# Attention probabilities scaled on VectorE or ScalarE instead of GpSimd, with a re-timed list schedule

## The chip, the cores and the metric

One core of a Trainium2 chip runs the whole kernel. The metric is the device time of one execution in microseconds (us); the time before is the median of three runs. The core's engines are TensorE (PE in the profile, its weight loads PEld), VectorE (DVE), ScalarE (ACT), GpSimd (POOL) and SyncE (SP), which issues most DMAs.

## The reference

Block-causal attention, then two MLPs over the same 2304 tokens, all in float32:

```python
# q, k, v: (4 batches, 8 heads, 576 positions, 64)
scores = scale * np.matmul(q, k.transpose(0, 1, 3, 2))
mask = block_i >= block_j                    # blocks of 64 positions
scores = np.where(mask, scores, -1000000000.0)
scores = scores - np.max(scores, axis=-1, keepdims=True)
attn = np.exp(scores)
attn = attn / (np.sum(attn, axis=-1, keepdims=True) + 1e-09)
x = np.matmul(attn, v)                       # -> (2304, 512)
h = x @ w_in;  r = np.maximum(h, 0.0);  g = s * (r * r) + b;  x = g @ w_out    # first MLP, d_ff 2048
h = x @ w_in2; g = np.maximum(0.01 * h, h);  out = g @ w_out2                  # second MLP, d_ff 2048
```

## The kernel before

The 576 positions are cut into five query tiles of 128 (the last one 64), over all four batches: tile `k` gives the first MLP a block of 512 tokens (tile 4: 256). They are taken in the order 0, 1, 2, 4, 3. While the first MLP works on one block (16 slices `f` of the hidden layer; `m_in` writes `h` with the matmuls of L910, `m_out` accumulates `y` with those of L953), the attention of the next block runs between its matmuls (`later_block`). So up to about 520 us TensorE has two streams of work; then the last block runs alone, and from about 592 us the second MLP, with seven products in place of eight for each pair of blocks (L1166 into the hidden layer, L1231 out of it).

Float32 matmuls of the MLPs are done as three with operands split into a high and a low part (`xh`, `xl`, `gh`, `gl`, and for weights `w`). VectorE and ScalarE split weights and activations, evacuate PSUM, and do the softmax. The weights of the second MLP are split and combined in slots named `unit` during the first one (L457 to L477).

One attention step of `later_block` takes one batch and one pair of heads, 16 steps for each of the four later tiles:

- TensorE: scores into PSUM (`s`; L577 for tile 1, L782 for tiles 2 and 3, L822 for tile 4).
- VectorE: row maximum; ScalarE: exponential with the sum of each row into `l`; VectorE: adds 1e-9 and takes the reciprocal (L556, L799, L840).
- The scaling, which multiplies each row of `P` by its value in `l`, in place: L569 for tile 1 (two instructions a step, 192 and 256 columns), L801 for tiles 2 and 3 (two a step, 384 or 512 columns), L841 for tile 4 (one a step, 576 columns). Before the change it may run on GpSimd or VectorE. Tile 0 scales on VectorE with a broadcast product (L562).
- TensorE: transposes of `P` in groups of four into `t` (L592); VectorE or ScalarE evacuates them into `pt`, part of the buffer `pv` (`evac`, L508 on ScalarE, L510 on VectorE); TensorE: the product with V (L861).

The order of all instructions on all engines is written out by a list scheduler in the kernel's own code, class `Graph`. Each operation is added as a step with the engines that may run it and a duration on each (`act`, `dve`, `pool`), its predecessors, the buffers that it opens and uses, and a due time. `Graph.order` simulates the engines: whenever an engine is idle in this simulation it takes the ready step with the earliest due time. Steps are then issued in the simulated order, and each engine works through its own queue in order; what waits at run time waits by semaphore. `LAT` is the time from a step's end until those who wait for it are ready in the simulation, `AGAIN` by how much an engine is free earlier than its step's end, `TURN` the cost on TensorE of a change between full, row-tiled and column-tiled matmuls. Steps marked `port` on VectorE and GpSimd exclude each other in the simulation.

Of the kernel before, what the change touches and what calls it, by code (L numbers as in the profile page):

```python
# [43 lines left out]
class Graph:  # L44
    LAT = 0.04
    AGAIN = {"DVE": 0.08, "ACT": 0.09, "POOL": 0.05}
# [8 lines left out]
    def add(self, eng, fn, after=(), opens=(), uses=(), due=0.0, port=False, nbytes=0, rel=0.0, mode="f", behind=(), run=2048):  # L55
        s = Step(eng, fn, after, opens, uses, due, port, nbytes)
        s.rel = rel
        s.mode = mode
        s.wire = nbytes / abs(run) * (12.0 + abs(run) / 23.0) / 16e3
# [31 lines left out]
    def order(self):  # L91
# [17 lines left out]
        while events:  # L109
            t = events[0][0]  # L110
            while events and events[0][0] <= t:
                _, _, what, s, e = heapq.heappop(events)
                if what == "ready":
                    for x in s.eng:
                        ready[x].append(s)
                elif what == "room":
                    room[s] += 1
                elif what == "free":
                    idle[e] = True
                    if port is s:  # L120
                        port = None
                else:
                    out_there -= s.nbytes > 0
                    for b in s.uses:
                        b.users -= 1
                        if not b.users:
                            heapq.heappush(events, (t + self.LAT, n, "room", b.key, None))
                            n += 1
                    for q in s.succs:
                        q.left -= 1  # L130
                        if not q.left:
                            heapq.heappush(events, (max(t + (0.18 if "POOL" in q.eng and len(q.eng) == 1 else self.LAT), q.rel), n, "ready", q, None))
                            n += 1
            for e in idle:
# [71 lines left out]
def kernel(  # L206
# [135 lines left out]
    def decode(raw, w0, w1, out, n, after, due):  # L342
# [10 lines left out]
        a = G.add({"DVE": dve(n, 2)}, low, after, uses=[raw], due=due, port=True)  # L353
        b = G.add({"ACT": act(n)}, up, after, uses=[raw], due=due)
        return G.add({"DVE": dve(n)}, shift, [a, b], uses=[raw], due=due, port=True)

    def chunk(w, raw, f, lds, halves, due):
# [13 lines left out]
        a = G.add({"DVE": dve(512 * n)}, lo, [a], uses=[w, raw], due=due, port=True)  # L371
# [53 lines left out]
    def units(which, stored):  # L425
# [4 lines left out]
        for n, (half, kind, i) in enumerate(seq[first[which]:first[which + 1]]):  # L430
# [34 lines left out]
            a = G.add({"DVE": dve(1024, 2)}, low, lds, uses=[slot], due=due, port=True)  # L465
            b = G.add({"ACT": act(1024)}, up, lds, uses=[slot], due=due)
            a = G.add({"DVE": dve(1024)}, shift, [a, b], uses=[slot], due=due, port=True)

            def comb(out, x, y, op, after, blk=blk, slot=slot, due=due):
                return G.add({"DVE": dve(256)}, lambda e: e.tensor_tensor(out=blk(out), in0=blk(x), in1=blk(y), op=op), after, uses=[slot], due=due, port=True)  # L470
# [6 lines left out]
            lo = G.add({"DVE": dve(1792)}, lambda e, c7=c7, h7=h7: e.tensor_tensor(out=c7(), in0=c7(), in1=h7(), op=ALU.subtract), [hi], uses=[slot], due=due, port=True)  # L477
# [43 lines left out]
    def softmax(k, banks, cols, P, pcols, due, after):  # L521
# [36 lines left out]
        if k == 0:  # L558
            for j in range(0, ns, 4):
# [4 lines left out]
                out += [G.add({"DVE": dve(n)}, fn, [a], uses=[P, l], due=due - 2.5, port=True)] * 4  # L564
            return out
        for j, (bk, c, n) in enumerate(cols):
            def fn(e, j=j, n=n):
                pp = P()[:, pcols[j]:pcols[j] + n]
                e.tensor_scalar(out=pp, in0=pp, scalar1=l()[:, j:j + 1], scalar2=1.0, op0=ALU.mult, op1=ALU.mult)  # L569
            out.append(G.add({"POOL": pool(n), "DVE": dve(n, 2)}, fn, [a], uses=[P, l], due=due - 2.5, port=True))  # L570
        return out

    def scores(k, q, kk, cols, q_ap, k_ap, after, due, fresh):
        out = []
        for j, (bk, c, n) in enumerate(cols):
# [4 lines left out]
            out.append(G.add({"PE": max(n * 1.67e-3, 0.214) - 0.06}, fn, after, new, [bk, *q, *kk], due - 5))  # L580
# [78 lines left out]
    for p in range(NP):  # L659
# [26 lines left out]
        a = G.add({"PE": 0.208 * 4}, av, [*tr, fv_ok, pads], [o], [pt, fv] + [spare] * (p > 1), due, mode="c")  # L686
# [14 lines left out]
    def score_parts(Q, K, nk, ql, kl, due):  # L701
# [7 lines left out]
            out=kl_()[:, :nk], in0=K()[:, :nk], in1=kh()[:, :nk].bitcast(F32), op=ALU.subtract), [c], [kl_], [K, kh], due=due - 7, port=True)  # L709
        return kh, kl_, qs, [a, c]  # L710

    def later_block(blk):
# [8 lines left out]
        for u in range(NP * B):  # L721
# [48 lines left out]
            if flat:  # L770
# [16 lines left out]
                for h in range(2):  # L787
# [7 lines left out]
                    for h in range(2)  # L795
# [16 lines left out]
            else:  # L812
# [6 lines left out]
                for j in range(2):  # L819
# [21 lines left out]
                nrm = [G.add({"POOL": pool(nk), "DVE": dve(nk, 2)}, lambda e, l=l, P=P: e.tensor_scalar(  # L841
                    out=P()[:, :nk], in0=P()[:, :nk], scalar1=l()[:, 0:1], scalar2=1.0, op0=ALU.mult, op1=ALU.mult), [a], uses=[P, l], due=due - 2.5, port=True)]
# [27 lines left out]
            a = G.add({"PE": many * nj * 0.206 * n / 128}, av, [x for c in pair for x in c[3]], [o] + [xf] * (pair[0][0] == 0), [xf, *[x for c in pair for x in (c[2], c[4])]], due, mode="c")  # L870
# [12 lines left out]
    def x_split(blk, c):  # L883
# [10 lines left out]
            [hi], [l], [h, xf], due, port=True,  # L894
# [5 lines left out]
    def m_in(blk, f, pos):  # L900
# [19 lines left out]
        def square(e):  # L920
# [9 lines left out]
            out=gl()[:, :T], in0=g()[:, :T], in1=gh()[:, :T].bitcast(F32), op=ALU.subtract), [hi], [gl], [g, gh], due, port=True)  # L930
# [112 lines left out]
    x2 = {}  # L1043

    def x_part(j, r, x, after, t):
# [3 lines left out]
        x2[j, r][2] = a = G.add({"DVE": dve(2 * NH)}, lambda e: sub(e, lo(), x(), hi().bitcast(F32)), [a], [lo], [hi, x.buf], t, port=True)  # L1049
# [26 lines left out]
    def x_comb(x, y, z, after, t):  # L1076
        return G.add(tt(2 * NH), lambda e: sub(e, x(), y(), z()), after, [], [x.buf, y.buf, z.buf], t, port=True)
# [110 lines left out]
    def out_phase(n):  # L1188
# [13 lines left out]
        for o, r in enumerate(IN_ORDER):  # L1202
            z, first = where[r]
            for i in range(4):
# [5 lines left out]
                def comb(x, y, w, after):  # L1210
                    return G.add(tt(NH), lambda e: sub(e, x(), y(), w()), after, [], [x, y, w], due - 4, port=True)
# [13 lines left out]
                lo = G.add({"DVE": dve(NH)}, lambda e, gh=gh, gl=gl, x=x: sub(e, gl(), x(), gh().bitcast(F32)), [hi], [gl], [gh, x], due - 1.5, port=True)  # L1225
# [101 lines left out]
```

## Time and profile before

| | |
|---|---|
| median of 3 runs | 957.47 us (957.29 to 958.84) |
| the profiled execution's own time | 957.85 us |
| its span, first to last instruction | 956.1 us |
| TensorE busy | 939.0 us (98%) |
| VectorE, ScalarE, GpSimd busy | 67%, 58%, 11% |
| mean granted TensorE clock | 0.998 |

The profile comes from one execution; durations and waits below are those of that execution. Busy time of TensorE is the time covered by at least one matmul; matmuls are pipelined and their ends are modelled, so one matmul's shown duration runs on over the start of the next. A weight load (PEld) overlaps the matmul in front of it. A wait is idle time of an engine, put down to what ended it.

### The profile page before, as it was taken

How to read it: one execution, taken by the hardware profiler on the slowest of the kernel's cores; microseconds unless marked ns; L12 is line 12 of the kernel's file. 1: busy time of each engine (PE TensorE's matmuls, PEld its weight loads, DVE VectorE, ACT ScalarE, POOL GpSimd, SP SyncE). 2: the span in 40 equal slices, each digit the busy share in tenths (PEclk: the TensorE clock that was granted, in tenths of full speed). 3: DMA queues.
4: the chain of work that ended last, by engine and by line, in shares of the span. 5: the costliest groups of instructions: out<-in, count | busy, mean ns of one | idle time of the engine just before them, and what ended most of it. 6: DMA issues, size and time to landing. Idle time of an engine off the chain costs nothing.

```text
span 956.1 us, 16595 instructions
## 1 busy us (share of the span) xinstructions
PE 939.0 (98%) x5780; PEld 827.9 (87%) x5780; DVE 635.9 (67%) x1300; ACT 559.0 (58%) x1186; POOL 101.4 (11%) x223
## 2 busy tenths in 40 slices
PE   9999999999999999999999999999999999999998
PEld 8778787777778888888887888999999999999998
DVE  5977668866768756666676754556595565855557
ACT  4867657656766745565567643454556646555443
POOL 1122211211121211121220000000000000000000
PEclk9999999999999999999999999999999999999999
DMA  8986677998679885178336992997219852157402
GB/s 226 322 294 221 233 256 249 313 281 243 186 217 336 223 261 173 47 247 236 100 103 206 387 332 87 360 418 322 97 57 322 316 189 99 51 177 292 165 1 67
DMA packets 147668, 208.27 MB, mean 218 GB/s; under 512 B 23552, under 2 KB 118400, under 8 KB 140928
## 3 DMA queue, kind: packets, MB, share of 16 engines
q1 hardware_dynamic: 145136, 206.42, 65.0%
q10 hardware_dynamic: 2448, 0.79, 0.4%
q8 instruction: 46, 0.75, 0.3%
q14 instruction: 38, 0.31, 0.1%
HBM read 154.47 MB, written 52.69 MB: 217 GB/s over the span
## 4 chain that ended last, share of the span: by engine, by line
PE 80%; DMA 6%; DVE 6%; ACT 3%; issue 2%; POOL 2%; SPq 0%; POOLq 0%; DVEq 0%; ACTq 0%
PE y L953 16%; PE h L910 15%; PE A L1231 10%; PE A L1166 10%; PE C L1166 5%; PE C L1231 5%; PE t L592 4%; PE o L861 4%; PE B L1231 3%; PE B L1166 2%; DMA pv<-in_v_dram 2%; PE s L577 2%; PE s L782 2%; PE warm L614 1%; DMA u_in<-unit 1%
## 5 line engine op out<-in xcount | busy, mean ns | idle before, releaser
L910 PE MATMUL h<-xh,w 128*128 128x512 f32 (+1 forms) x640 | 231.5, 388 | 1.7 <-DVE g L924 1.0
L953 PE MATMUL y<-gh,w 128*128 128x512 f32 (+1 forms) x640 | 187.4, 376 | 0.2
L910 PEld LDWEIGHTS h<-xh,w 128*128 128x128 f32 x640 | 119.2, 189 | 28.2 <-issue 5.1
L953 PEld LDWEIGHTS y<-gh,w 128*128 128x128 f32 x640 | 114.0, 189 | 21.3 <-issue 0.9
L1224 ACT ACTIVATE gh<-G 128x384 fp32r<-128x384 f32 x168 | 86.9, 525 | 55.4 <-PE A L1231 21.0
L953 PE MATMUL y<-gl,w 128*128 128x512 f32 (+1 forms) x320 | 118.7, 371 | 0.1
L910 PE MATMUL h<-xl,w 128*128 128x512 f32 (+1 forms) x320 | 118.7, 371 | 0.0
L1166 PE MATMUL A<-xh,wi 128*128 128x384 f32 x384 | 112.4, 336 | 0.0
L1038 DVE TENSOR_TENSOR gl<-G,gh 128x384 fp32r<-128x384 f32 x168 | 91.3, 555 | 29.9 <-ACT gh L1224 28.2
L1231 PE MATMUL A<-gh,wo 128*128 128x384 f32 x384 | 98.0, 336 | 1.4 <-DVE Y L1146 1.4
L926 ACT ACTIVATE g<-h 128x512 f32<-128x512 f32 (+1 forms) x80 | 44.2, 552 | 91.3 <-PE h L910 91.2
L592 PE MATMUL t<-id_sb,p 128*128 128x128 f32 x400 | 68.6, 280 | 8.1 <-POOL p L569 2.7
L592 PEld LDWEIGHTS t<-id_sb,p 128*128 128x128 f32 x400 | 46.6, 140 | 30.6 <-POOL p L569 6.4
L1166 PEld LDWEIGHTS A<-xh,wi 128*128 128x128 f32 x384 | 70.6, 188 | 1.1 <-ACT G L1141 0.9
L1231 PEld LDWEIGHTS A<-gh,wo 128*128 128x128 f32 x384 | 69.1, 188 | 2.4 <-DVE Y L1146 2.3
L953 PEld LDWEIGHTS y<-gl,w 128*128 128x128 f32 x320 | 60.4, 189 | 11.1 <-DVE gl L929 0.7
L929 DVE TENSOR_TENSOR gl<-g,gh 128x512 fp32r<-128x512 f32 (+1 forms) x80 | 53.2, 664 | 22.8 <-ACT gh L928 17.3
L910 PEld LDWEIGHTS h<-xl,w 128*128 128x128 f32 x320 | 60.7, 190 | 7.3
L1180 ACT ACTIVATE G<-G 128x384 f32<-128x384 f32 x72 | 37.6, 524 | 47.8 <-DVE G L1146 47.7
L1166 PE MATMUL A<-xl,wi 128*128 128x384 f32 x192 | 64.4, 335 | 0.0
L1231 PE MATMUL A<-gl,wo 128*128 128x384 f32 x192 | 64.2, 334 | 0.0
L1038 DVE TENSOR_TENSOR G<-G 128x384 f32<-128x384 f32 x96 | 53.1, 555 | 12.3 <-ACT G L1180 10.8
(123 smaller groups left out, 1797.2 us busy)
## 6 DMA issues: line engine op xcount, KB each, us to landing
wi<-u_in SPq DMA_DIRECT2D x32, 896.0 KB, 7.1
wo<-u_out SPq DMA_DIRECT2D x28, 1024.0 KB, 7.4
w<-kept SPq DMA_DIRECT2D x16, 1024.0 KB, 8.0
u_in<-unit SPq DMA_DIRECT2D x16, 896.0 KB, 5.4
u_out<-unit SPq DMA_DIRECT2D x32, 448.0 KB, 5.3
early<-in_moe_w_in_dram SPq DMA_DIRECT2D x16, 512.0 KB, 5.4
early<-in_moe_w_out_dram SPq DMA_DIRECT2D x16, 512.0 KB, 6.4
kept<-w SPq DMA_DIRECT2D x8, 1024.0 KB, 6.6
```

Of the source, the lines that this page charges most:

```text
L577: e.matmul(out=bk()[:, c:c + n], lhsT=q_ap(j), rhs=k_ap(j, n), start=True, stop=True)
L592: e.transpose(tb()[:, x * 128:(x + 1) * 128], P()[:, pc:pc + 128], id_sb)
L861: e.matmul(out=o()[64 * h:64 * h + 64, n * x:n * x + n], lhsT=V()[:, j, 64 * h:64 * h + 64], rhs=r, start=(j == 0), stop=(j == nj - 1),)
L910: e.matmul(out=h()[:, :T], lhsT=w()[:, wi, c * 128:(c + 1) * 128], rhs=x[blk, c]()[:, :T], start=(c == 0 and n == 0), stop=(c == KD - 1 an ...
L926: a = G.add({"ACT": act(T)}, lambda e: e.activation(out=g()[:, :T], in_=h()[:, :T], func=ACTF.Relu), [prev], [g], [h], due)
L929: lo = G.add({"DVE": dve(T)}, lambda e: e.tensor_tensor(out=gl()[:, :T], in0=g()[:, :T], in1=gh()[:, :T].bitcast(F32), op=ALU.subtract), [ ...
L953: e.matmul(out=y()[:, :W], lhsT=w()[:, wi, d * 128:(d + 1) * 128], rhs=x()[:, :W], start=(pos == 0 and n == 0), stop=(pos == NF - 1 and n ...
L1038: e.tensor_tensor(out=out, in0=x, in1=y, op=ALU.subtract)
L1166: e.matmul(out=x()[:, :NH], lhsT=in_w[n, i, c]()[:, s, ai], rhs=y()[:, c], start=(first and c == 0 and m == 0), stop=(c == 1 and m == 2), ...
L1180: {"ACT": act(NH)}, lambda e, y=y: e.activation(out=y(), in_=y(), func=ACTF.Prelu, alpha=0.01), [a], [], [y], d2 + 2)
L1224: hi = G.add({"ACT": act(NH)}, lambda e, gh=gh, x=x: e.activation(out=gh(), in_=x(), func=ACTF.Copy), [a], [gh], [x], due - 2)
L1231: e.matmul(out=z[d]()[:, :NH], lhsT=out_w[n, r]()[:, 2 * i + d, s], rhs=y(), start=(first and i == 0 and m == 0), stop=(i == 3 and m == 2) ...
```

## The change

The scaling of tiles 1 to 4 no longer has GpSimd as a choice: it becomes `evac(e, P, P, l)`, which is a `tensor_scalar` with one multiplication on VectorE, or a Copy activation with `l` as its per-partition scale on ScalarE, with the durations of the new function `norm`. The scheduler takes whichever of the two is idle in its simulation. All `port=True` marks are dropped. In the scheduler, `LAT` depends on the engine that the waiting step goes to; a result of TensorE reaches other engines `LAG` later than it reaches TensorE's own next steps, which follow with no latency; a landed load counts 0.1 us; the durations of the score matmuls and of the products with V are longer. (`tail` is not set by any step.)

```diff
-    LAT = 0.04
-    AGAIN = {"DVE": 0.08, "ACT": 0.09, "POOL": 0.05}
+    LAT = {"PE": 0.055, "DVE": 0.035, "ACT": 0.035, "POOL": 0.17, "SP": 0.03, "X": 0.0}
+    LAG = 0.165
+    AGAIN = {"DVE": 0.08, "ACT": 0.095, "POOL": 0.03}
...
                         if not b.users:
-                            heapq.heappush(events, (t + self.LAT, n, "room", b.key, None))
+                            heapq.heappush(events, (t + 0.036, n, "room", b.key, None))
...
                     for q in s.succs:
+                        if e == "PE" and q.on_pe:
+                            continue
                         q.left -= 1
                         if not q.left:
-                            heapq.heappush(events, (max(t + (0.18 if "POOL" in q.eng and len(q.eng) == 1 else self.LAT), q.rel), n, "ready", q, None))
+                            lat = 0.1 if s.nbytes and not q.nbytes else self.LAT[min(q.eng)]
+                            heapq.heappush(events, (max(t + lat, q.rel), n, "ready", q, None))
...
+                if e == "PE":
+                    for q in s.succs:
+                        if q.on_pe:
+                            q.left -= 1
+                            if not q.left:
+                                heapq.heappush(events, (max(end, q.rel), n, "ready", q, None))
+                                n += 1
+                    end += self.LAG
+                elif e in ("ACT", "DVE") and s.tail:
+                    end += s.tail
...
 def act(n, ptr=0, acc=False):
-    return 0.2 + n / 1200 + 0.14 * acc
+    return 0.205 + n / 1195 + 0.125 * acc
...
+def norm(n):
+    return {"DVE": 0.212 + n / 1840, "ACT": act(n) + 0.06}
...
                 pp = P()[:, pcols[j]:pcols[j] + n]
-                e.tensor_scalar(out=pp, in0=pp, scalar1=l()[:, j:j + 1], scalar2=1.0, op0=ALU.mult, op1=ALU.mult)
-            out.append(G.add({"POOL": pool(n), "DVE": dve(n, 2)}, fn, [a], uses=[P, l], due=due - 2.5, port=True))
+                evac(e, pp, pp, l()[:, j:j + 1])
+            out.append(G.add(norm(n), fn, [a], uses=[P, l], due=due - 2.5))
...
-            out.append(G.add({"PE": max(n * 1.67e-3, 0.214) - 0.06}, fn, after, new, [bk, *q, *kk], due - 5))
+            out.append(G.add({"PE": max(n * 1.67e-3, 0.19) + 0.005}, fn, after, new, [bk, *q, *kk], due - 5))
...
-        a = G.add({"PE": 0.208 * 4}, av, [*tr, fv_ok, pads], [o], [pt, fv] + [spare] * (p > 1), due, mode="c")
+        a = G.add({"PE": 0.218 * 4}, av, [*tr, fv_ok, pads], [o], [pt, fv] + [spare] * (p > 1), due, mode="c")
...
-                    G.add({"POOL": pool(nk), "DVE": dve(nk, 2)}, lambda e, h=h, l=l, P=P: e.tensor_scalar(
-                        out=P()[:, nk * h:nk * h + nk], in0=P()[:, nk * h:nk * h + nk], scalar1=l()[:, h:h + 1], scalar2=1.0, op0=ALU.mult, op1=ALU.mult),
-                        [a], uses=[P, l], due=due - 2.5, port=True)
+                    G.add(norm(nk), lambda e, h=h, l=l, P=P: evac(
+                        e, P()[:, nk * h:nk * h + nk], P()[:, nk * h:nk * h + nk], l()[:, h:h + 1]), [a], uses=[P, l], due=due - 2.5)
...
-                nrm = [G.add({"POOL": pool(nk), "DVE": dve(nk, 2)}, lambda e, l=l, P=P: e.tensor_scalar(
-                    out=P()[:, :nk], in0=P()[:, :nk], scalar1=l()[:, 0:1], scalar2=1.0, op0=ALU.mult, op1=ALU.mult), [a], uses=[P, l], due=due - 2.5, port=True)]
+                nrm = [G.add(norm(nk), lambda e, l=l, P=P: evac(
+                    e, P()[:, :nk], P()[:, :nk], l()[:, 0:1]), [a], uses=[P, l], due=due - 2.5)]
...
-            a = G.add({"PE": many * nj * 0.206 * n / 128}, av, [x for c in pair for x in c[3]], [o] + [xf] * (pair[0][0] == 0), [xf, *[x for c in pair for x in (c[2], c[4])]], due, mode="c")
+            a = G.add({"PE": many * nj * 2 * (0.109 if n == 128 else 0.058)}, av, [x for c in pair for x in c[3]], [o] + [xf] * (pair[0][0] == 0), [xf, *[x for c in pair for x in (c[2], c[4])]], due, mode="c")
```

The other lines of the diff only drop `port=True`, on the subtractions, combinations and weight decoding of VectorE.

## Rows read from the trace of the kernel before

**Rows 1.** The page: engines (busy us, share, instructions); its costliest group (busy, mean ns).

```profile
PE 939.0 (98%) x5780; PEld 827.9 (87%) x5780; DVE 635.9 (67%) x1300; ACT 559.0 (58%) x1186; POOL 101.4 (11%) x223
...
L910 PE MATMUL h<-xh,w 128*128 128x512 f32 (+1 forms) x640 | 231.5, 388 | 1.7 <-DVE g L924 1.0
```

**Rows 2.** Windows: length, busy us (instructions) of each engine, PEclk, DMA share, GB/s.

```profile
25.00:525.00 500.00, 489.25 (x3273) 395.39 (x3272) 356.71 (x795) 322.14 (x699) 96.67 (x205) 1.00 0.72 225
525.00:592.00 67.00, 67.00 (x297) 55.47 (x296) 39.60 (x55) 32.67 (x46) 0.00 (x0) 1.00 0.77 271
592.00:952.00 360.00, 358.63 (x2048) 355.23 (x2047) 225.38 (x421) 191.92 (x386) 0.00 (x0) 1.00 0.54 198
...
50.00:75.00 25.00, 22.86 (x123) 18.40 (x122) 18.95 (x35) 16.43 (x31) 5.49 (x12) 0.93 0.87 291
```

**Rows 3.** Waits of PE: who for whom, total us, times, longest.

```profile
PE t L592 <- POOL p L569: 2.7, 4, 1.6
PE t L592 <- POOL p L801: 2.5, 6, 0.8
...
PE h L910 <- DVE g L924: 1.0, 2, 0.6
...
PE t L592 <- ACT pv L508: 0.3, 1, 0.3
...
PE t L592 <- POOL p L841: 0.2, 1, 0.2
```

**Rows 4.** Waits of PEld, the weight loads, same columns.

```profile
PEld t L592 <- POOL p L569: 6.4, 12, 1.8
PEld t L592 <- POOL p L801: 6.1, 13, 1.0
...
PEld t L592 <- POOL p L841: 2.9, 8, 0.6
```

**Rows 5.** Groups of POOL by shape: count, busy us, mean ns, idle before, releasers.

```profile
L801 POOL TENSOR_SCALAR p<-p,l 128x512 f32<-128x512 f32 x31 | 22.1, 724 | 77.7 <-DVE l L799 65.5 <-ACT xh L891 6.9 <-PE h L910 5.3
L801 POOL TENSOR_SCALAR p<-p,l 128x384 f32<-128x384 f32 x32 | 22.1, 702 | 82.9 <-DVE l L799 57.1 <-ACT gh L928 19.1 <-ACT xf L508 6.7
L841 POOL TENSOR_SCALAR p<-p,l 128x576 f32<-128x576 f32 x16 | 13.6, 847 | 39.6 <-DVE l L840 38.3 <-ACT kh L707 1.3
L569 POOL TENSOR_SCALAR p<-p,l 128x192 f32<-128x192 f32 x15 | 10.1, 675 | 51.3 <-DVE l L556 39.8 <-ACT xh L891 6.0 <-ACT unit L460 4.9
L569 POOL TENSOR_SCALAR p<-p,l 128x256 f32<-128x256 f32 x16 | 10.0, 628 | 0.0
```

**Rows 6.** Lines 569 and 801 by themselves: ns min/median/max, first and last start.

```profile
L569 POOL TENSOR_SCALAR p<-p,l x31: 427/482/1965, 41.8 to 152.3; 128x256 f32<-128x256 f32 x16, 128x192 f32<-128x192 f32 x15
...
L801 POOL TENSOR_SCALAR p<-p,l x63: 582/694/1633, 158.5 to 506.2; 128x384 f32<-128x384 f32 x32, 128x512 f32<-128x512 f32 x31
```

**Rows 7.** Groups of DVE by shape: the two scalings that ran there.

```profile
L801 DVE TENSOR_SCALAR p<-p,l 128x512 f32<-128x512 f32 x1 | 0.5, 491 | 0.0
L569 DVE TENSOR_SCALAR p<-p,l 128x192 f32<-128x192 f32 x1 | 0.3, 312 | 0.0
```

**Rows 8.** Groups of ACT by shape: copies with a per-partition scale, out of PSUM.

```profile
L508 ACT ACTIVATE yo<-y,s_sb 128x512 f32<-128x512 f32 x8 | 5.5, 684 | 3.0 <-PE y L953 2.9
...
L508 ACT ACTIVATE yo<-y,s_sb 128x256 f32<-128x256 f32 x2 | 0.9, 460 | 0.0
```

**Rows 9.** Timeline from 54 us: start, us, engine and instruction, idle before it.

```profile
54.40 2.37 POOL L569 TENSOR_SCALAR p<-p,l 128x192 f32<-128x192 f32 x2 [4.65 <-DVE l L556]
54.67 1.23 DVE L367 TENSOR_TENSOR w<-early,w 128x1024 fp32r<-128x1024 f32 x1
...
56.83 0.55 PE L592 MATMUL t<-id_sb,p 128*128 128x128 f32 x3 [1.61 <-POOL p L569]
```

**Rows 10.** The chain that ended last, from 542 us: start, us, what.

```profile
542.87 3.40 PE h L910 x15
```

**Rows 11.** Groups of DVE by shape: the longest instruction of the weight split.

```profile
L477 DVE TENSOR_TENSOR unit<-unit 128x1792 f32<-128x1792 f32 x16 | 32.5, 2032 | 11.3 <-ACT unit L476 11.2
```

More of the change, by code (lines that the diff above doesn't have):

```diff
@@ L53, in __init__, with add @@
         self.room, self.inturn, self.steps, self.gates = room, inturn, [], {}
-    def add(self, eng, fn, after=(), opens=(), uses=(), due=0.0, port=False, nbytes=0, rel=0.0, mode="f", behind=(), run=2048):
+    def add(self, eng, fn, after=(), opens=(), uses=(), due=0.0, port=False, nbytes=0, rel=0.0, mode="f", behind=(), run=2048, tail=0.0):
         s = Step(eng, fn, after, opens, uses, due, port, nbytes)
@@ L58, in add @@
         s.mode = mode
+        s.on_pe = "PE" in eng
+        s.tail = tail
         s.wire = nbytes / abs(run) * (12.0 + abs(run) / 23.0) / 16e3
@@ L351, in shift @@
             e.scalar_tensor_tensor(out=out(), in0=w1(), scalar=3, in1=w0(), op0=ALU.logical_shift_left, op1=ALU.bitwise_or)
-        a = G.add({"DVE": dve(n, 2)}, low, after, uses=[raw], due=due, port=True)
+        a = G.add({"DVE": dve(n, 2)}, low, after, uses=[raw], due=due)
         b = G.add({"ACT": act(n)}, up, after, uses=[raw], due=due)
-        return G.add({"DVE": dve(n)}, shift, [a, b], uses=[raw], due=due, port=True)
+        return G.add({"DVE": dve(n)}, shift, [a, b], uses=[raw], due=due)
     def chunk(w, raw, f, lds, halves, due):
@@ L370, in chunk @@
         a = G.add({"ACT": act(512 * n)}, hi, [a, w_ok.get((0, f - 1, 0))], [w] * (halves[0] == 0), [w, raw], due)
-        a = G.add({"DVE": dve(512 * n)}, lo, [a], uses=[w, raw], due=due, port=True)
+        a = G.add({"DVE": dve(512 * n)}, lo, [a], uses=[w, raw], due=due)
         for i in halves:
@@ L476, in units @@
             hi = G.add({"ACT": act(1792)}, lambda e, c7=c7, h7=h7: e.activation(out=h7().bitcast(F32R), in_=c7(), func=ACTF.Copy), [s3, s4], uses=[slot], due=due)
-            lo = G.add({"DVE": dve(1792)}, lambda e, c7=c7, h7=h7: e.tensor_tensor(out=c7(), in0=c7(), in1=h7(), op=ALU.subtract), [hi], uses=[slot], due=due, port=True)
+            lo = G.add({"DVE": dve(1792)}, lambda e, c7=c7, h7=h7: e.tensor_tensor(out=c7(), in0=c7(), in1=h7(), op=ALU.subtract), [hi], uses=[slot], due=due)
             st = []
@@ L563, in softmax @@
                 n = 4 * cols[j][2]
-                out += [G.add({"DVE": dve(n)}, fn, [a], uses=[P, l], due=due - 2.5, port=True)] * 4
+                out += [G.add({"DVE": dve(n)}, fn, [a], uses=[P, l], due=due - 2.5)] * 4
             return out
@@ L708, in score_parts @@
         c = G.add({"DVE": dve(nk)}, lambda e: e.tensor_tensor(
-            out=kl_()[:, :nk], in0=K()[:, :nk], in1=kh()[:, :nk].bitcast(F32), op=ALU.subtract), [c], [kl_], [K, kh], due=due - 7, port=True)
+            out=kl_()[:, :nk], in0=K()[:, :nk], in1=kh()[:, :nk].bitcast(F32), op=ALU.subtract), [c], [kl_], [K, kh], due=due - 7)
         return kh, kl_, qs, [a, c]
@@ L893, in x_split @@
             {"DVE": dve(T)}, lambda e: e.tensor_tensor(out=l()[:, :T], in0=xf()[:, :T], in1=h()[:, :T].bitcast(F32), op=ALU.subtract),
-            [hi], [l], [h, xf], due, port=True,
+            [hi], [l], [h, xf], due,
         )
@@ L929, in m_in @@
         lo = G.add({"DVE": dve(T)}, lambda e: e.tensor_tensor(
-            out=gl()[:, :T], in0=g()[:, :T], in1=gh()[:, :T].bitcast(F32), op=ALU.subtract), [hi], [gl], [g, gh], due, port=True)
+            out=gl()[:, :T], in0=g()[:, :T], in1=gh()[:, :T].bitcast(F32), op=ALU.subtract), [hi], [gl], [g, gh], due)
         if k == NB - 1:
@@ L1210, in comb @@
                 def comb(x, y, w, after):
-                    return G.add(tt(NH), lambda e: sub(e, x(), y(), w()), after, [], [x, y, w], due - 4, port=True)
+                    return G.add(tt(NH), lambda e: sub(e, x(), y(), w()), after, [], [x, y, w], due - 4)
                 x, a = {1: (g11, ok[1, 1]), 2: (g21, ok[2, 1]), 3: (g22, ok[2, 2])}.get(r, (None, None))
@@ L1224, in out_phase @@
                 hi = G.add({"ACT": act(NH)}, lambda e, gh=gh, x=x: e.activation(out=gh(), in_=x(), func=ACTF.Copy), [a], [gh], [x], due - 2)
-                lo = G.add({"DVE": dve(NH)}, lambda e, gh=gh, gl=gl, x=x: sub(e, gl(), x(), gh().bitcast(F32)), [hi], [gl], [gh, x], due - 1.5, port=True)
+                lo = G.add({"DVE": dve(NH)}, lambda e, gh=gh, gl=gl, x=x: sub(e, gl(), x(), gh().bitcast(F32)), [hi], [gl], [gh, x], due - 1.5)
                 q[r] = lo
```

10 lines of the change are left out of this document (5 added, 5 removed).

## Prediction

> **What bounds the kernel now.** I read the page first. Its top line says how full each engine is [rows 1]: TensorE (PE) works 939.0 of 956.1 us, VectorE (DVE) 67%, ScalarE (ACT) 58%, GpSimd (POOL) 11%. So TensorE is the bound and at most 17.1 us of idle time can be won from it, plus whatever it loses by running slowly. Next the windows [rows 2]: in the stretch 25:525, where attention and the first MLP are mixed, TensorE is idle for 500 - 489.25 = 10.75 us; in the second MLP (592:952) for 1.4 us. All of GpSimd's scaling lies in the first stretch. The change is won or lost there. That stretch has DVE at 71% and ACT at 64%, so neither is full, but neither is free at any moment.
>
> The waits of TensorE tell who makes it idle [rows 3]. Four waits for the scaling in L569 (tile 1), six for L801 (tiles 2 and 3) and one for L841 (tile 4) add up to 2.7 + 2.5 + 0.2 = 5.4 us: half of the stretch's idle time. Six rows, from DVE g to ACT pv, are waits for the other two engines, 3.7 us in all. The same view for weight loads [rows 4] shows 33 waits for the scaling, 6.4 + 6.1 + 2.9 = 15.4 us, 0.47 us each. The truth lies between 5.4 and 15.4: a matmul of L910 is shown with 388 ns [rows 1], but 15 of them take 3.40 us [rows 10], 0.227 each, so about 0.16 us of each shown matmul lies over the next one, and a stall shorter than that is not seen as idle time. I count the 11 seen waits as 0.16 longer (7.2 us) and the other 22 as 0.08 each (1.8 us): **9.0 us of stall**.
>
> One such stall is to be seen whole [rows 9]. Two scalings of tile 1 start at 54.40 and take 2.37 us, while VectorE runs a subtraction with two inputs from 54.67. TensorE stands for 1.61 us in the midst of four transposes, until the second scaling is done. The window 50:75 is the only one in the stretch with a granted clock under 1.00 [rows 2]: 0.93, which is 3.4 us at the lower of the two levels and costs 25 x 0.07 = 1.7 us. It falls right behind this stall.
>
> **The change, part by part.**
>
> *Scaling leaves GpSimd.* 110 instructions there took 77.9 us [rows 5]. Their prices on the two new engines: two scalings happened to run on VectorE already, 192 columns in 0.312 and 512 in 0.491 us [rows 7], a line of 0.56 ns per column, so 256, 384 and 576 cost 0.348, 0.419 and 0.527. ScalarE's nearest row is a copy scaled by a per-partition value from PSUM, 0.684 us for 512 and 0.460 for 256 [rows 8]: 0.40, 0.57 and 0.74 for 192, 384 and 576. Over the counts of rows 5 that is 47.3 us if all go to VectorE, 64.8 if all go to ScalarE. A pair of 384 columns took 1.40 us on GpSimd, one behind the other; on VectorE it takes 0.84, on both engines side by side 0.57. The chain from reciprocal to transpose is 0.56 to 0.83 us shorter, against a mean stall of 0.47 and longest ones of 1.8, 1.0 and 0.6. For a 576-column row it is only 0.11 to 0.32 shorter. Both ends: nothing gained if the new place in the queue eats it, 9.0 if all goes. I take 80%: **-7.2 us**.
>
> *The clock.* If the stall at 54.9 goes, the drop behind it should go. Between 0 and -1.7, and below nothing if another hole opens in the first 60 us; I take **-1.2**.
>
> *More work on VectorE and ScalarE.* With half on each, VectorE in 25:525 goes from 356.7 to 380.4 us (idle share 28.7 to 23.9%), ScalarE from 322.1 to 354.5 (35.6 to 29.1%). What queues behind a scaling there are the row maxima, the subtractions for the low halves, the PSUM evacuations and the exponentials; TensorE waits for those. Waits that grow as the idle share shrinks make 3.7 x 0.22 = 0.8 us: the lower end. The upper end is that scalings themselves sit behind long instructions: the weight split has instructions of 2.03 us on VectorE [rows 11]. With 64 softmaxes (16 for each of four tiles), 0.2 us for each makes 12.8 us. The first end is nearer, since a wait for the evacuations of transposes, which stand in the same queues, hardly shows now (0.3 us for ACT pv, [rows 3]). I take **+2.0**.
>
> *Planner.* Taking `port` away moves no instruction by itself; the planner merely no longer holds VectorE back while it believes GpSimd scales. The new `LAG` of 0.165 us for results of TensorE is what [rows 10] shows as the tail of a matmul, and TensorE's own successors now follow at once in the plan. So the order written out should leave fewer places where TensorE runs into a result that is not there. It can also come out worse, since all five engine queues, and SP's DMA issues with them, are ordered anew. Bounds: the 10.75 - 5.4 = 5.35 us of idle time that is not GpSimd's, either way. I take **-1.5**. The changed durations for scores and AV products alter no instruction and go into this term.
>
> *At no cost:* GpSimd keeps its memsets and casts, at 11% busy before; with no scaling ahead of them, the zeroed q tiles and the loads behind them on SP can only be ready earlier, and no wait of TensorE for those tiles stands among its waits. The second MLP has no GpSimd work [rows 2] and 1.4 us idle, so only the planner's term can reach it.
>
> Sum against the profiled execution's own 957.85 us: -7.2 - 1.2 + 2.0 - 1.5 = -7.9, so 949.95. That execution lies 0.38 above the median of 957.47; on the median's scale the forecast is **949.6 us**.
>
> **Rivals.**
>
> *A, larger gain.* The plan fits so well that all stalls for GpSimd, the clock drop and the other idle time of the stretch go: 957.85 - 9.0 - 1.7 - 5.35 + 0.8 - 0.38 = 942.2. For it: the idle time in 525:592, where the same two matmul groups run without attention, is nil [rows 2]. Against it: attention's dependent steps remain.
>
> *B, no change to speak of.* The stall changes its owner. On GpSimd the scaling itself is not slow when undisturbed: at its quickest 0.427 us (192 columns) and 0.582 (384) [rows 6], only 0.12 and 0.16 above VectorE's price, so a pair is 0.3 us shorter, half of the 9.0 goes, and the new queues take 3.5 of it back: 957.85 - 4.5 + 3.5 - 0.38 = 956.5. For it: the quickest ones; against it: the mean is 0.675 and 0.702 [rows 5] and the longest 1.965, so undisturbed is not the case here. The Trainium skill (GPSIMD Engine Reference, section Engine selection) states that GpSimd runs single-input elementwise work at roughly line rate, and is about twice as slow for two inputs. By that rule this single-input scaling would gain little by moving, which is this rival; the trace agrees for the quickest (0.582 us for 384 columns) and not for the mean.
>
> *C, slower.* Scalings are queued in order behind the weight split, and the four transposes behind them stand. VectorE's instructions of 2.03 us come sixteen times [rows 11], and there are shorter ones of the same kind on both engines; on GpSimd nothing stood in front. It decides from (7.2 + 1.2 + 1.5) / 64 = 0.155 us of added stall for each softmax; at 0.2 us it costs 12.8 in place of 2.0, and the time is 949.6 + 10.8 = 960.4. Against it: the planner knows these durations and gives the scaling an early due time.
>
> That the change doesn't do what it says is no rival here: the new entry has no GpSimd in it. Only the share between VectorE and ScalarE is open; all on ScalarE would bring its stretch to 77% and leads to C.
>
> **How the numbers follow.** Forecast 0.52, A 0.14, B 0.18, C 0.16. A measurement tells about 0.2% (1.9 us) from no change. The likeliest case by itself reaches from 945.5 (planner's term at -5.35) to 954.5 (half of the stall stays, and the clock drop). The range for all is 943 to 959: it leaves out half of A and most of C, some 0.18. Faster: forecast and A, 0.66; same: B, 0.18; slower: C, 0.16.
>
> **What the profile of the changed kernel would show.** No row of GpSimd for the scaling; 110 rows of it on VectorE and ScalarE near 0.42 and 0.57 us for 384 columns. TensorE's waits for the scaling under 1.5 us in all, weight loads' under 4. Idle time of TensorE in 25:525 near 5 us instead of 10.75, and a clock of 1.00 in 50:75. TensorE's waits for VectorE and ScalarE there up from 3.7 to about 5 or 6. The forecast is wrong if those go past 8, if the clock drops in more windows, or if the second MLP's idle time, which nothing here touches, moves by more than 2 us.

## The result and the profile after

The changed kernel takes 944.51 us (median of 4, 944.32 to 946.81) against 957.45: a ratio of 0.9867, 95% interval 0.9849 to 0.9885, so 12.9 us less. Forecast were 949.6 us, with 943 to 959 as the range. Its line numbers are 19 or 20 higher from L569 on: L592 is now L612, L910 is L929, L953 is L972.

The page's first line and three windows of the changed kernel's profile (columns as in [rows 1] and [rows 2]; this execution took 944.63 us, its span is 942.8):

```profile
PE 929.3 (99%) x5780; PEld 828.4 (88%) x5780; DVE 660.3 (70%) x1374; ACT 576.8 (61%) x1222; POOL 26.1 (3%) x113
```

```profile
25.00:525.00 500.00, 492.79 (x3322) 405.96 (x3321) 387.22 (x875) 344.20 (x742) 21.33 (x95) 1.00 0.75 234
...
25.00:50.00 25.00, 22.48 (x123) 17.68 (x122) 22.67 (x44) 21.42 (x47) 1.24 (x5) 0.93 1.01 334
50.00:75.00 25.00, 25.00 (x144) 20.79 (x143) 23.59 (x45) 19.64 (x39) 1.54 (x7) 1.00 0.94 311
```

TensorE's idle time in 25:525 fell from 10.75 to 7.2 us, its busy time over the whole span from 939.0 to 929.3. The same 5780 matmuls cannot have become shorter; the second number is stalls too short to show as idle, as the prediction warned of [rows 1, 10]. One group holds both kinds. First the transposes of the kernel before, then those of the changed one (busy us, mean ns | idle before, and what ended it):

```profile
L592 PE MATMUL t<-id_sb,p 128*128 128x128 f32 x400 | 68.6, 280 | 8.1 <-POOL p L569 2.7 <-POOL p L801 2.5 <-DVE p L562 0.9
```

```profile
L612 PE MATMUL t<-id_sb,p 128*128 128x128 f32 x400 | 64.2, 275 | 2.7 <-ACT xf L528 1.0 <-DVE p L532 0.9 <-ACT pv L528 0.5
```

Busy and idle together, the transposes go from 76.7 to 66.9 us: **9.8 of the 12.9 us** sit there. This count misses a stall that lies under the shown tail of the group in front. Taken from starts (the distance from the start of the matmul in front to the start of a transpose, less the usual distance for the same two shapes, the lower quartile over all runs), the delay ahead of transposes goes from 17.5 to 5.5 us: 12.0 of the 13.2 us between the two profiles. What TensorE waits for now (the same columns as [rows 3]):

```profile
PE h L929 <- DVE g L943: 1.9, 2, 1.0
...
PE h L929 <- DVE xl L710: 1.3, 1, 1.3
PE h L929 <- ACT g L945: 1.0, 1, 1.0
PE t L612 <- ACT xf L528: 1.0, 1, 1.0
PE t L612 <- DVE p L532: 0.9, 2, 0.5
```

No wait for GpSimd's scaling is left; of the 5.4 us that were shown, 0.9 are now waits for a scaling on VectorE, while waits for VectorE and ScalarE in all rose from 3.7 to 6.8 us. The scalings by shape (count, busy us, mean ns):

```profile
L532 DVE TENSOR_SCALAR p<-p,l 128x384 f32<-128x384 f32 x22 | 8.7, 417 | 0.4
...
L532 DVE TENSOR_SCALAR p<-p,l 128x576 f32<-128x576 f32 x13 | 6.8, 520 | 0.6
L528 ACT ACTIVATE p<-p,l 128x384 f32<-128x384 f32 x10 | 6.1, 612 | 2.0 <-DVE l L819 2.0
```

69 scalings are on VectorE and 43 on ScalarE. VectorE's prices are those that the prediction drew through two points (0.419 and 0.527 us); ScalarE's 0.612 is 0.04 over its estimate.

In the profiled execution the clock did not come back. It is 1.00 in 50:75 now, but 0.93 in 25:50, the same 1.7 us at another place, again in a timeline with two holes (start, us, instruction, idle before):

```profile
36.33 0.50 PE L929 MATMUL h<-xl,w 128*128 128x512 f32 x1 [1.26 <-DVE xl L710]
...
38.87 0.79 PE L929 MATMUL h<-xh,w 128*128 128x512 f32 x1 [1.05 <-DVE g L943]
39.46 0.63 PE L929 MATMUL h<-xl,w 128*128 128x512 f32 x1
```

The matmul at 36.33 still took 0.50; those from 38.87 on are shown with 0.6 to 0.8 where 0.39 is usual. But this is one execution of four. Its mean granted clock is 0.998 and it took 944.63 us; the other three have 1.000 and took 944.32, 944.40 and 946.81. Of 43 executions of the kernel before that ran beside the experiments, 36 have 0.997 or 0.998 (957.5 us in the median) and only five 1.000 (954.5). So in three of four executions the clock drop of before is gone, though no time shows what it costs the changed kernel.

### The profile page after: what moved, and what is told of

Its sections match the earlier page's. It is cut to its first block, busy times and chain, and to the rows that moved or that the text cites. A ratio compares the mean times of both kernels' runs of the same rounds, so it can differ in the third digit from the quotient of the medians.

```text
span 942.8 us, 16507 instructions
## 1 busy us (share of the span) xinstructions
PE 929.3 (99%) x5780; PEld 828.4 (88%) x5780; DVE 660.3 (70%) x1374; ACT 576.8 (61%) x1222; POOL 26.1 (3%) x113
## 4 chain that ended last, share of the span: by engine, by line
PE 91%; DVE 4%; DMA 2%; ACT 1%; issue 1%; SPq 1%; ACTq 0%; DVEq 0%
PE y L972 21%; PE h L929 21%; PE A L1250 10%; PE A L1185 10%; PE C L1185 5%; PE C L1250 5%; PE o L880 4%; PE t L612 4%; PE B L1250 3%; PE s L802 3%; PE B L1185 2%; PE s L597 1%; PE s L841 1%; DMA fk<-in_k_dram 1%; DMA early<-in_moe_w_in_dram 1%
## 5 line engine op out<-in xcount | busy, mean ns | idle before, releaser
L929 PE MATMUL h<-xh,w 128*128 128x512 f32 (+1 forms) x640 | 209.9, 385 | 3.0 <-DVE g L943 1.9
L972 PE MATMUL y<-gh,w 128*128 128x512 f32 (+1 forms) x640 | 187.9, 377 | 0.1
L929 PEld LDWEIGHTS h<-xh,w 128*128 128x128 f32 x640 | 118.6, 189 | 29.5 <-DVE g L943 3.8
L972 PEld LDWEIGHTS y<-gh,w 128*128 128x128 f32 x640 | 112.9, 189 | 20.6 <-issue 2.4
L929 PE MATMUL h<-xl,w 128*128 128x512 f32 (+1 forms) x320 | 118.8, 371 | 1.3 <-DVE xl L710 1.3
L972 PE MATMUL y<-gl,w 128*128 128x512 f32 (+1 forms) x320 | 118.5, 370 | 0.0
L1250 PEld LDWEIGHTS A<-gh,wo 128*128 128x128 f32 x384 | 69.2, 188 | 2.3 <-DVE Y L1165 2.3
L972 PEld LDWEIGHTS y<-gl,w 128*128 128x128 f32 x320 | 60.3, 188 | 10.8 <-DVE gl L948 0.5
L948 DVE TENSOR_TENSOR gl<-g,gh 128x512 fp32r<-128x512 f32 (+1 forms) x80 | 50.7, 634 | 26.4 <-ACT gh L947 25.8
L929 PEld LDWEIGHTS h<-xl,w 128*128 128x128 f32 x320 | 60.8, 190 | 9.5 <-DVE xl L710 1.7
L612 PE MATMUL t<-id_sb,p 128*128 128x128 f32 x400 | 64.2, 275 | 2.7 <-ACT xf L528 1.0
L612 PEld LDWEIGHTS t<-id_sb,p 128*128 128x128 f32 x400 | 47.7, 140 | 18.0 <-issue 4.4
```

Of the source, the lines that this page charges most:

```text
L612: e.transpose(tb()[:, x * 128:(x + 1) * 128], P()[:, pc:pc + 128], id_sb)
L929: e.matmul(out=h()[:, :T], lhsT=w()[:, wi, c * 128:(c + 1) * 128], rhs=x[blk, c]()[:, :T], start=(c == 0 and n == 0), stop=(c == KD - 1 an ...
L948: lo = G.add({"DVE": dve(T)}, lambda e: e.tensor_tensor(out=gl()[:, :T], in0=g()[:, :T], in1=gh()[:, :T].bitcast(F32), op=ALU.subtract), [ ...
L972: e.matmul(out=y()[:, :W], lhsT=w()[:, wi, d * 128:(d + 1) * 128], rhs=x()[:, :W], start=(pos == 0 and n == 0), stop=(pos == NF - 1 and n ...
L1250: e.matmul(out=z[d]()[:, :NH], lhsT=out_w[n, r]()[:, 2 * i + d, s], rhs=y(), start=(first and i == 0 and m == 0), stop=(i == 3 and m == 2) ...
```

## The experiments

All times are medians, each with its ratio to runs of the kernel before on the same chip. "Transposes" is busy plus idle of their group, "changes" the number of times that TensorE goes over between the matmul groups of h and y, "lost" the sum over all runs of like matmuls of the distance from their first start to the next run's first start, less their number times the usual distance of that kind (0.227 us for 512 columns, 0.109 for a transpose): TensorE's stalls and turns of all lengths. These three columns come from the one profiled execution of each kernel, which can lie some us from its median: most of all with LAG 0.150, profiled at 948.05 us with a clock of 0.86 in 25:50.

| kernel | us | ratio, 95% | transposes | changes | lost |
|---|---|---|---|---|---|
| before | 957.45 | | 76.7 | 290 | 53.5 |
| changed | 944.51 | 0.9867 (0.9849 to 0.9885) | 66.9 | 93 | 40.3 |
| scaling only | 952.53 | 0.9950 (0.9935 to 0.9966) | 68.5 | 266 | 47.7 |
| plan only | 953.45 | 0.9966 (0.9948 to 0.9984) | 74.2 | 96 | 47.4 |
| order of before, VectorE | 948.95 | 0.9911 (0.9895 to 0.9926) | 69.2 | 290 | 44.8 |
| the same, scaling twice | 962.88 | 1.0064 (1.0050 to 1.0078) | 82.3 | 290 | 59.7 |
| before, PE at once | 967.16 | 1.0105 (1.0086 to 1.0124) | 78.3 | 95 | 61.3 |
| changed, VectorE only | 953.96 | 0.9966 (0.9954 to 0.9978) | 69.0 | 91 | 51.8 |
| changed, LAG 0 | 951.81 | 0.9947 (0.9928 to 0.9966) | 67.6 | 104 | 45.2 |
| changed, not at once | 946.32 | 0.9891 (0.9874 to 0.9907) | 65.8 | 260 | 43.5 |
| changed, LAG 0.150 | 943.85 | 0.9871 (0.9852 to 0.9891) | 67.2 | 95 | 43.7 |
| changed, LAG 0.180 | 944.93 | 0.9882 (0.9862 to 0.9901) | 65.9 | 93 | 38.9 |
| order of changed, GpSimd | 969.49 | 1.0133 (1.0110 to 1.0156) | 88.1 | 93 | 63.3 |
| order of changed, VectorE | 946.95 | 0.9893 (0.9875 to 0.9911) | 68.5 | 93 | 41.9 |

Theory 1 was that the stall belongs to GpSimd: the scaling's length and place there. Theory 2: it belongs to the plan, which took TensorE's results as ready too early and put too little between a scaling and its transposes.

**One half each.** Scaling only: the diff's scaling part on the old scheduler.

```diff
-            out.append(G.add({"POOL": pool(n), "DVE": dve(n, 2)}, fn, [a], uses=[P, l], due=due - 2.5, port=True))
+            out.append(G.add(norm(n), fn, [a], uses=[P, l], due=due - 2.5))
...
-        a = G.add({"DVE": dve(n, 2)}, low, after, uses=[raw], due=due, port=True)
+        a = G.add({"DVE": dve(n, 2)}, low, after, uses=[raw], due=due)
```

> The scaling runs on VectorE or ScalarE and the port marks are gone, with the scheduler's constants of before. Theory 1, the stall belongs to GpSimd: the 9 us of stall at the transposes go almost whole here too, so 9 to 11 us under before, and TensorE's waits for the scaling are under 1.5 us. Theory 2, the plan does it (it takes TensorE's results as later and puts other work in between): 0 to 4 us under before. Either way the number of changes between the matmul groups of h and y stays as in before (290).

It gave 4.9 us, less than theory 1 asked for and more than theory 2, and the changes fell to 266, where 290 had been expected. The transposes did lose 8.2 us; the new order gave 3.3 back elsewhere, most of it in the wait for the square of h, which holds TensorE's next slice back (one row of TensorE's waits; [rows 3] has 1.0 for it):

```profile
PE h L913 <- DVE g L927: 4.4, 5, 1.4
```

Plan only: `Graph`, `act` and the durations of scores and AV products as in the changed kernel, the scaling on GpSimd.

```diff
-    LAT = 0.04
+    LAT = {"PE": 0.055, "DVE": 0.035, "ACT": 0.035, "POOL": 0.17, "SP": 0.03, "X": 0.0}
+    LAG = 0.165
...
-            out.append(G.add({"PE": max(n * 1.67e-3, 0.214) - 0.06}, fn, after, new, [bk, *q, *kk], due - 5))
+            out.append(G.add({"PE": max(n * 1.67e-3, 0.19) + 0.005}, fn, after, new, [bk, *q, *kk], due - 5))
```

> The scheduler and the durations are those of after, the scaling stays on GpSimd with its port marks. Theory 1: 2 to 4 us under before, with TensorE's waits for GpSimd's scaling still near 5 us. Theory 2: 9 us or more under before, with those waits under 2 us. The changes between the groups of h and y fall from 290 to about 95 in both.

4.0 us by the medians, 3.3 by the ratio, as theory 1 had it, and the waits for GpSimd's scaling are all still there (6.0 us):

```profile
PE t L608 <- POOL p L585: 4.7, 6, 1.3
...
PE t L608 <- POOL p L817: 1.0, 3, 0.4
...
PE t L608 <- POOL p L857: 0.3, 1, 0.3
```

The halves add up to 8 or 9 us; together they give 12.9. Each half also got an order of everything of its own, so the two numbers hold more than the halves.

**The order held.** To take the replanning out, the scheduler is left as in before, and what it had put on GpSimd is issued on VectorE at the same place.

```diff
-                e.tensor_scalar(out=pp, in0=pp, scalar1=l()[:, j:j + 1], scalar2=1.0, op0=ALU.mult, op1=ALU.mult)
+                e = nc.vector
+                e.tensor_scalar(out=pp, in0=pp, scalar1=l()[:, j:j + 1], scalar2=1.0, op0=ALU.mult, op1=ALU.mult)
```

> The order of all instructions is that of before; only the scalings that stood in GpSimd's queue are issued on VectorE, at the same place in the order. Theory 1: the chain from reciprocal to transpose is shorter and undisturbed, 5 to 8 us under before. Theory 2: without a new order nothing is gained, within 2 us of before. Rival C of the prediction (scalings stand behind long instructions of VectorE): slower than before by 2 us or more.

8.5 us faster, with every other instruction where it was: theory 1, even a little over its 5 to 8, and against rival C. The stall of [rows 9] in this kernel's timeline, its window, and its transposes:

```profile
54.23 0.67 DVE L570 TENSOR_SCALAR p<-p,l 128x192 f32<-128x192 f32 x2
...
54.79 0.72 PE L593 MATMUL t<-id_sb,p 128*128 128x128 f32 x4 [0.68 <-DVE p L570]
```

```profile
50.00:75.00 25.00, 24.32 (x138) 19.66 (x137) 22.64 (x47) 18.63 (x35) 1.39 (x6) 1.00 0.98 313
```

```profile
L593 PE MATMUL t<-id_sb,p 128*128 128x128 f32 x400 | 65.7, 278 | 3.5 <-DVE pv L510 0.9 <-DVE p L562 0.9 <-DVE p L570 0.7
```

The two scalings take 0.67 in place of 2.37 us, TensorE waits once for 0.68, and here the clock does stay up, with a mean of 1.000 in all four executions. The transposes lose 7.5 us, and 1.7 for the clock makes 9.2, about the whole.

The reverse: the order of the changed kernel, with the scalings on GpSimd.

```diff
-                evac(e, pp, pp, l()[:, j:j + 1])
+                nc.gpsimd.tensor_scalar(out=pp, in0=pp, scalar1=l()[:, j:j + 1], scalar2=1.0, op0=ALU.mult, op1=ALU.mult)
```

> The order of the changed kernel, with its 112 scalings issued on GpSimd at the same places. If GpSimd's place and length make the stall, 8 to 12 us slower than the changed kernel (953 to 957), with TensorE's waits for GpSimd's scaling over 5 us again. If the new order leaves room behind each scaling, within 3 us.

25 us slower than the changed kernel, twice what theory 1 had expected, and 12 slower than before:

```profile
PE t L612 <- POOL p L821: 7.1, 14, 1.3
PE t L612 <- POOL p L589: 5.7, 5, 1.4
PE t L612 <- POOL p L859: 2.6, 5, 1.1
```

```profile
L612 PE MATMUL t<-id_sb,p 128*128 128x128 f32 x400 | 70.4, 281 | 17.7 <-POOL p L821 7.1 <-POOL p L589 5.7 <-POOL p L859 2.6
```

21.2 of the 25 us are in the transposes. The same order that gains with the scalings on VectorE and ScalarE loses 12 us with them on GpSimd. My reading is that an order planned for a short scaling puts the transposes close behind it, so it has more to lose with a long one; that would also be why the two halves, each tried alone, add up to less than the whole.

**Is it the length?** The order of before on VectorE, with a product by 1.0 ahead of each scaling.

```diff
+                nc.vector.tensor_scalar(out=pp, in0=pp, scalar1=1.0, scalar2=1.0, op0=ALU.mult, op1=ALU.mult)
                 e.tensor_scalar(out=pp, in0=pp, scalar1=l()[:, j:j + 1], scalar2=1.0, op0=ALU.mult, op1=ALU.mult)
```

> As the run with the order of before and all scalings on VectorE, but each scaling is preceded by a product of the same columns with 1.0, so that a pair of 384 columns takes 1.66 us where GpSimd took 1.40 and VectorE 0.84. The values are the same. If the length of the scaling in the chain is what made the stall on GpSimd, most of the 8.6 us go again: 953 to 957. If it was the hop to GpSimd, or TensorE waits little for the chain's length, 949 to 951. Over 958 the load on VectorE itself would be the price.

13.9 us slower than the same with one scaling, and over 958, the case that had been kept for the load on VectorE. The transposes account for 13.1 of it, mostly by waits for the scaling itself:

```profile
L594 PE MATMUL t<-id_sb,p 128*128 128x128 f32 x400 | 69.5, 281 | 12.8 <-DVE p L803 5.0 <-DVE pv L510 2.3 <-DVE p L571 1.5
```

TensorE's waits for a scaling of these tiles rose from 0.7 to 7.1 us, those for evacuations, which queue behind it, by 2.5 (DVE pv and ACT pv). A scaling can be late by its own length or by the longer queue in front of it, so chain and load are not told apart beyond that. There is little slack: as much VectorE work again as the scalings took costs 14 us of time.

**Which share on which engine?**

```diff
-    return {"DVE": 0.212 + n / 1840, "ACT": act(n) + 0.06}
+    return {"DVE": 0.212 + n / 1840}
```

> The changed kernel with the scaling on VectorE alone (43 of 110 were on ScalarE). If the share on ScalarE is what keeps the new waits low, slower than the changed kernel by 2 us or more, with more waits for VectorE's g; if a scaling behind its own reciprocal on VectorE is the shorter chain, 0 to 2 us faster. In between nothing is told.

9.5 us slower than the changed kernel. Before taking that as the worth of ScalarE's share, the order of the changed kernel was kept and the 43 scalings were issued on VectorE:

```diff
-                evac(e, pp, pp, l()[:, j:j + 1])
+                nc.vector.tensor_scalar(out=pp, in0=pp, scalar1=l()[:, j:j + 1], scalar2=None, op0=ALU.mult)
```

> The order of the changed kernel, with all scalings issued on VectorE at the same places (43 of them were on ScalarE). If the share on ScalarE itself is worth the 9.5 us that the run with the scaling on VectorE alone lost, 6 to 10 us slower than the changed kernel; if that loss came from the other order of everything else, within 3 us.

Only 2.4 us, with overlapping intervals. So about 7 of the 9.5 us are what the scheduler made of having one engine less. This run also pairs with the one that held the order of before: all scalings are on VectorE in both, so the new order by itself gives 948.95 - 946.95 = 2.0 us, again with overlapping intervals. Its transposes stand between those of that run and those of the changed kernel:

```profile
L612 PE MATMUL t<-id_sb,p 128*128 128x128 f32 x400 | 64.8, 276 | 3.7 <-ACT xf L528 1.4 <-DVE p L589 0.8 <-ACT pv L528 0.5
```

In the replanned run with VectorE only the transposes are fine (69.0 us), and the losses are elsewhere:

```profile
PE h L929 <- DVE g L943: 3.4, 3, 2.0
PE h L929 <- ACT g L945: 2.0, 1, 2.0
```

**Which part of the plan?** First on the old scheduler, TensorE's own next step ready at the end of the one before:

```diff
+                if e == "PE":
+                    for q in s.succs:
+                        if q.on_pe:
+                            q.left -= 1
+                            if not q.left:
+                                heapq.heappush(events, (max(end, q.rel), n, "ready", q, None))
+                                n += 1
                 heapq.heappush(events, (end, n, "done", s, e))
```

> The scheduler of before in which a step of TensorE makes TensorE's next step ready at its end instead of 0.04 us later; nothing else. If the many changes between the groups of h and y cost time, this alone gives 2 to 3 us and the number falls to about 95; if they cost nothing, within 1 us of before.

The number of changes fell as expected, and the time rose by 9.7 us: a clear miss, since neither outcome had it. The clock is lower in two windows, 0.14 x 25 = 3.5 and 1.75 us:

```profile
275.00:300.00 25.00, 20.67 (x121) 16.12 (x120) 20.56 (x41) 12.95 (x28) 4.41 (x10) 0.86 0.85 269
...
500.00:525.00 25.00, 22.98 (x179) 19.81 (x179) 18.35 (x40) 17.51 (x37) 5.45 (x12) 0.93 0.34 109
```

and the waits for GpSimd and for g are longer:

```profile
PE t L602 <- POOL p L811: 4.5, 4, 2.3
PE h L920 <- DVE g L934: 3.5, 3, 1.8
```

Then the two parts of the changed scheduler by themselves.

```diff
-    LAG = 0.165
+    LAG = 0.0
```

> The changed kernel with LAG = 0, so that the plan again takes TensorE's results as ready at its end, while TensorE's own next steps still follow at once. If the lag is what makes the new plan worth something: 4 to 9 us slower than the changed kernel (949 to 954), the same sign as following at once had by itself on the old scheduler. If the lag does nothing: within 1.5 us of the changed kernel.

7.3 us slower than the changed kernel in the median. Of six executions three have a mean clock of 1.000 (949.6 to 951.0 us) and three of 0.994 or 0.995 (952.6 to 954.1), so some 5 us are stalls and the rest goes with the clock. The profiled one is the fastest (949.55). There the wait for g doubles; the transposes' busy and idle time is nearly that of the changed kernel (67.6 us), but taken from starts the delay ahead of them is 9.1 us in place of 5.5:

```profile
PE h L929 <- DVE g L943: 3.9, 5, 1.8
```

```diff
-                                heapq.heappush(events, (max(end, q.rel), n, "ready", q, None))
+                                heapq.heappush(events, (max(end + 0.04, q.rel), n, "ready", q, None))
```

> The changed kernel, but TensorE's next step gets ready 0.04 us after the end of the one before, as it was before; the lag stays. The changes between the groups of h and y go from about 93 back to 250 or more. If these cost nothing, within 2 us of the changed kernel; if they cost, 2 to 3 us slower.

1.8 us slower, with an interval that overlaps the changed kernel's: 260 changes instead of 93 are worth little or nothing. Of these two parts of the plan it is the lag that counts; the new latencies by engine and the new durations were not tried by themselves. A likely reason, not shown by a run: 12 matmuls of one slice in a row end in a result that the plan without lag expects 0.165 us too early.

**How much is luck?** `LAG = 0.150` and `LAG = 0.180` change the plan and nothing else.

> The changed kernel with LAG = 0.150 in place of 0.165: no instruction is added or taken away, only the plan differs a little. If a plan's exact order is worth several us by itself, 2 to 6 us from the changed kernel, more likely slower (the changed kernel's order would then be a lucky one); if the plans are good in the mean, within 1.5 us.

> The changed kernel with LAG = 0.180: the same question from the other side, and whether more lag does better than 0.165. Scatter of plans: 2 to 6 us from the changed kernel; none: within 1.5 us.

943.85 and 944.93: within 0.7 us of the changed kernel, so its order is no lucky one among its neighbours. No version that was run is told apart from it as faster.

## Why the prediction was right, and what was mis-sized

*The forecast as a whole.* The time lies 1.5 us above the lower end of the range. It is 5.1 us under the forecast and under the 945.5 to which the likeliest case was said to reach (its own terms make 945.7), so the mechanism was hit better than the size.

*The bound and the place.* Right. 9.8 of 12.9 us come from the transposes that waited for GpSimd; the second MLP's idle time moved by less than 1 us.

*Scaling leaves GpSimd, -7.2.* Right, in mechanism and size: with the order held the transposes lost 7.5 us of the 9.0 that I had counted by adding the overlap of matmuls to the shown waits. In the changed kernel it is 9.8.

*The clock, -1.2.* Right where the order was held (1.00 in 50:75, so the whole 1.7 us). In the changed kernel three of four executions have no drop; the profiled one has the same 1.7 us behind two other holes before 39 us, which the prediction had named as a way to lose it.

*More work on VectorE and ScalarE, +2.0.* Too high where the order was held: 7.5 us from the transposes and 1.7 from the clock make 9.2, the time fell by 8.5, so 0.7 is left for this term. In the changed kernel the waits shown rose by 3.1 us, but 0.9 of that is for the scaling, and 1.3 is a wait for `xl` that the plan-only run, with the scaling on GpSimd, has as well. That long instructions in front of the scaling would decide (rival C) did not come true: in the old order, with all scalings in VectorE's queue, the time fell. Its mechanism is real all the same, since scalings of double length there make the kernel slower than before.

*The planner, -1.5, and the 5.1 us between forecast and result.* The three terms of the scaling make -6.4 in the forecast and measured -8.5 with the order held and all scalings on VectorE; the load counted too high makes 1.3 of these 2.1 us, the clock 0.5, the transposes 0.3. From there the changed kernel is another 948.95 - 944.51 = 4.4 us faster, against 1.5 forecast. That is not all the planner's, since 43 of its scalings are on ScalarE: with all on VectorE the new order gives 2.0 us, and ScalarE's share the other 2.4. Both steps have overlapping intervals, so their sum is firm and the split is not. By this split the planner was sized about right (within the bounds of 5.35 that stood beside it), and what was mis-sized is the scaling on two engines: -6.4 in the forecast, -10.9 measured if its parts are added.

I took the plan as one small term beside the scaling and did not see that they depend on each other: the same order costs 12 us when the scaling is on GpSimd, and the scaling's move from GpSimd to VectorE is worth 8.5 us in the old order and 969.49 - 946.95 = 22.5 in the new one. The 4.4 us lie ahead of the transposes too: the delay taken from starts is 17.5 us before, 9.8 with the order held, 7.5 with the new order on VectorE and 5.5 in the changed kernel. Busy plus idle time shows 2.3 of them (69.2 to 66.9).

Rival A, all of the stage's idle time, comes nearer to the result (942.2, so 2.3 us off) than the forecast (5.1 off), but is not what happened: 7.2 us of idle time are left. Rival B's condition, that the scaling on GpSimd is undisturbed, does not hold (below).

## What to carry to other kernels

A dependent step off the bottleneck engine is priced by its latency, disturbances included, and an engine at 11% can be the one that the bottleneck waits for. When a change goes through a scheduler that reorders everything, hold the order and swap the engine alone, and hold the engine and swap the order: a part tried with a fresh plan (VectorE only cost 9.5 us with a fresh plan, 2.4 with the changed kernel's order kept) says as much about the plan as about the part. Stalls shorter than the shown tail of a matmul are counted as busy; take the busy and the idle time of one group together, or better the distances from start to start, which also see what lies under the tail of the group in front.

## What the runs showed of the hardware

A scaling on GpSimd and some instructions of VectorE hold each other up. In the trace of before, 20 of the 110 scalings take over 0.1 us more than usual, 12.0 us in all (usual are 0.427, 0.480, 0.590, 0.690 and 0.750 us for 192 to 576 columns). Each of the 20 lies beside a VectorE instruction with two inputs in SBUF or beside a `tensor_scalar` of 192 columns or more from SBUF to SBUF; the 64 that lie beside neither take at most 0.013 us more. The 23 that lie beside more than 0.5 us of tensor-tensor or scalar-tensor-tensor work take 0.44 us more in the mean, up to 1.5, though ten of them at most 0.03. A second input in PSUM does not do it: in the changed order on GpSimd, 24 scalings met VectorE's product `g<-g,h` (`h` is in PSUM) and nothing else of the kind, for up to 0.46 us, and took at most 0.008 us more.

This is much of what the change takes away. Of the 5.4 us that TensorE is shown to wait for GpSimd's scaling in the kernel before, 3.9 stand behind scalings held up by over 0.1 us; in the changed order on GpSimd it is 13.1 of 15.4. Two pairs of 192 and 256 columns, in the timeline of the changed order on GpSimd:

```profile
60.29 2.37 POOL L589 TENSOR_SCALAR p<-p,l 128x192 f32<-128x192 f32 x2 [3.72 <-DVE l L576]
...
68.93 0.88 POOL L589 TENSOR_SCALAR p<-p,l 128x192 f32<-128x192 f32 x2 [4.53 <-ACT g L943]
```

With an order planned for a short scaling such meetings got more frequent (28 of 112 scalings), and the mean for 256 columns rose from 0.628 to 0.910 us:

```profile
L589 POOL TENSOR_SCALAR p<-p,l 128x256 f32<-128x256 f32 x16 | 14.6, 910 | 0.0
```

VectorE can be the one that stands instead. In the kernel before, this subtraction of 256 columns, usually 0.42 us, began 0.07 us after a scaling had begun and took 0.90, while the two scalings beside it took no longer than usual; the same is seen four times between 461 and 500 us:

```profile
461.24 0.90 DVE L929 TENSOR_TENSOR gl<-g,gh 128x256 fp32r<-128x256 f32 x1 [0.61 <-POOL p L801]
```

The Trainium skill (GPSIMD Engine Reference, section Specifications) says that GpSimd shares its SBUF interfaces with VectorE and contends with instructions that have two SBUF inputs or run in a two-port mode. These runs agree for two SBUF inputs and give it a size, 0.44 us in the mean of those 23; whether the `tensor_scalar` ones ran in a two-port mode no trace shows. It is also why the skill's rule of roughly line rate for single-input work (the Trainium skill, GPSIMD Engine Reference, section Engine selection), on which rival B stood, held for the undisturbed scalings at most: 0.590 us against 0.417 on VectorE for 384 columns, and 0.702 with the disturbed ones.

The clock's drops are not bound to one stall. In the first 75 us of their profiles the changed kernel had one behind holes of 1.26 and 1.05 us and the kernel before behind one of 1.61. The run with LAG 0.180 had none, with a hole of 1.7 us among its waits, and neither had the plan-only run, LAG 0 and the changed order on VectorE, with nearly the same two holes as the changed kernel (1.25 or 1.26 and 1.04). What decides between these was not tried.
